# A Fourier filter and a snake MLP on one core: padded alpha rows, more filler matmuls in the head, a denser batch 1, and stores on a third queue

## The chip, the cores and the metric

The kernel runs on 1 core of one Trainium2 chip. The metric is the device time of one execution in microseconds (us), as the median of several runs; lower is better. A core has five engines that run their own instruction streams in order and wait for each other by semaphores: PE (matmuls; its weight loads are shown as PEld), DVE and ACT (element-wise work), POOL (element-wise work, and it issues DMAs) and SP (it only issues DMAs here).

## The reference

`x` holds 8 batches of 3008 rows with 256 channels. The first half filters each channel along the rows in the frequency domain, the second half is an MLP with the snake activation:

```python
X = np.fft.rfft(x, axis=1)
F = (filt_r + 1j * filt_i)[None, :, :]
y = np.fft.irfft(X * F, n=3008, axis=1)
h = y.reshape(24064, 256) @ w_in            # 256 -> 2048
s = np.sin(alpha * h)
g = h + s * s / (alpha + 1e-09)
out = g @ w_out                             # 2048 -> 256
```

Inputs and output are float32.

## The kernel before, in words

**The filter.** The transform of 3008 = 47 x 64 points is done by matmuls in four stages. `first` (L177, tiles `pa`, matmul L180) multiplies by the 47-point table; its result goes through DRAM (`d1`, stored on SP's queue at L185, loaded on POOL's at L192). `forward` (L195, tiles `pb`) multiplies by the 64-point table; ACT copies the result to `xf` (L203). `product` (L210, DVE, L214) and `cross` (L218, DVE, L220 and L221) multiply by the filter; `cross` needs `xs`, the copy of `xf` with its halves swapped, which two DMAs on SP's queue make (L207). `inverse` (L223, tiles `pc`, matmul L231) goes back; its results `g` are stored to `d2` on SP's queue (L238), and `load_t4` (L241, SP's queue, L243) reads them again in another order. `last` (L246, tiles `pd`, matmuls L255 for batch 0 and L258 for the others) ends the transform and leaves `y`, with channels on partitions. There are 12 units `u` of forward, product, cross and inverse, and 16 of `first` and `last`, for each of the 8 batches. `evac` (L156) copies a PSUM tile, on ACT (L159) or DVE (L161): where the caller doesn't say, by turns, two on ACT and one on DVE.

**The MLP.** `hidden` (L498) takes a chunk of up to 512 columns of `y` and one of 16 blocks of 128 hidden channels: two matmuls (L505, tile `ph`, four PSUM buffers), a cosine on ACT (L508), and on DVE `v = cos - 1 - ph` (L509). With `w_in` multiplied by alpha and `w_out` by -1/(2 alpha) beforehand this is the snake. `project` (L513) multiplies `v` by `w_out` (matmuls L521, tile `po`); ACT copies the result to `o` (L527), and `store` (L536) writes rows of `o` to DRAM in two to seven DMAs (L546).

**The order.** There are 48 chunks; batches go in pairs. The main loop (L617) has 8 steps for each chunk and one more chunk's worth at the end: a step issues two `hidden` of chunk k, then whatever of the filter is due, then the `project` units of chunk k-1. What is due is a list `pending` (L552): every piece of the filter is put there with a due time in steps (`put`, L554), sorted, and `slot` (L594) issues what is due, at most one PE piece at a time unless it is a step late. A piece's due time is thus the only thing that says where it lands in each engine's stream.

**The head.** Batch 0's filter is done in a way of its own before the main loop, in an order written by hand (L359 to L490), with the DRAM trips replaced by DVE transposes (`turn`, L381, L383). Three details matter here:

- `spread_alpha` (L293) brings alpha, split by POOL into three bf16 parts (`split_alpha`, L284), to all 128 partitions by matmuls (L298): 12 for each of four tiles, called twice in pairs, as early as L377 and again at L481. `one` and `part` have 16 rows.
- `warm_pe(n)` (L347) issues n matmuls of 128x512 on a tile of zeros (L352). Nothing reads their result.
- The last head pieces are `s0.last(0)`, `(2)`, `(1)`, `(3)`. The first two read `t4_h[0]`, which `turn_back(0)` writes on DVE, the other two `t4_h[1]` from `turn_back(1)`. Eight matmuls make one piece. Chunk 0 needs all four.

```python
    spread_alpha(2)
    spread_alpha(3)
    for step in ([(weights_in, g) for g in range(6)] + [(s1.load_x, 0), (s1.load_x, 1)]):
        step[0](*step[1:])
    warm_pe(2)
    s0.last(0, True)
    s0.last(2, True)
    warm_pe(1)
    s0.last(1, True)
    s0.last(3, False)
```

**The end.** The last chunk has four blocks of 128 columns. Blocks 0 and 1 leave together; blocks 2 and 3 (`final`) are copied and stored alone. SP's queue carries all stores, but for the last two blocks the second piece of a run goes to ACT's queue (L539).

Of the kernel before, what the change touches and what calls it, by code (L numbers as in the profile page):

```python
# [11 lines left out]
BF16 = mybir.dt.bfloat16  # L12
UINT32 = mybir.dt.uint32
AFT = mybir.ActivationFunctionType
ALU = mybir.AluOpType
# [47 lines left out]
def kernel(  # L63
# [10 lines left out]
    nc = tc.nc  # L74
# [17 lines left out]
    def pool(name, bufs, space=None):  # L92
        kw = {} if space is None else {"space": space}
        return ctx.enter_context(tc.tile_pool(name=name, bufs=bufs, **kw))

    cpool = pool("consts", 1)
# [27 lines left out]
    for h in range(2):  # L124
        nc.sync.dma_start(out=x32[:, 4 * C * h:4 * C * h + 4 * C],
                          in_=bass.AP(tensor=x.tensor, offset=x.offset + 4 * h * C, ap=[[32 * C, 96], [1, 4 * C]]))
# [145 lines left out]
    id32 = cpool.tile([16, 16], FP32)  # L272
# [5 lines left out]
    nc.gpsimd.dma_start(out=id16, in_=id16_dram.ap())  # L278
    e1_0 = by_half(t4_h[1])
    rest = cpool.tile([16, 128], FP32)  # L280
    parts = [cpool.tile([16, 128], BF16, name=f"part{i}") for i in range(3)]
    one = cpool.tile([16, 16], BF16)

    def split_alpha():  # L284

        nc.gpsimd.tensor_copy(out=one, in_=id32)
        for i, part in enumerate(parts):
            src = rest if i else al
            nc.gpsimd.tensor_copy(out=part, in_=src)
            if i < 2:  # L290
                nc.gpsimd.tensor_tensor(out=rest, in0=src, in1=part, op=ALU.subtract)

    def spread_alpha(i):  # L293

        ps = hps.tile([128, 4, 128], FP32, name=f"al_bc_{i}", tag="h")
        for a in range(4):
            for k, part in enumerate(parts):
                nc.tensor.matmul(out=ps[:, a, :], lhsT=one[:, 4 * i + a:4 * i + a + 1].to_broadcast([16, 128]),  # L298
                                 rhs=part, start=(k == 0), stop=(k == 2))
        nc.scalar.copy(out=alpha[:, i // 2, 512 * (i % 2):512 * (i % 2) + 512], in_=ps.rearrange("p a b -> p (a b)"))  # L300

    for g in range(2):
        gs = slice(12 * g, 12 * g + 12)
        for k, filt in enumerate((filt_r, filt_i)):
            for q in range(2):
                if (g, k, q) == (0, 1, 1):
                    split_alpha()
                off, step = ((12 * g) * C, C) if q == 0 else ((N1 - 12 * g) * C, -C)
                marks["filt", g, k] = nc.gpsimd.dma_start(
                    out=f_t[k][64 * k + 32 * q:64 * k + 32 * q + 32, gs, :],  # L310
                    in_=bass.AP(tensor=filt.tensor, offset=filt.offset + off,
                                ap=[[N1 * C, 32], [step, 12], [1, C]]))
        nc.gpsimd.dma_start(out=e_t[:, gs, :], in_=e_dram.ap()[:, gs])
# [33 lines left out]
    def warm_pe(n):  # L347

        warmed.append(n)
        ps = hps.tile([128, 512], FP32, name=f"warm_{len(warmed)}", tag="h")  # L350
        for i in range(n):
            nc.tensor.matmul(out=ps, lhsT=idle[:, 0:128], rhs=idle[:, 0:512], start=True, stop=True)  # L352
# [13 lines left out]
    for i in range(16):  # L366
        own, tag = (fps, "f") if i % 3 == 2 else (hps, "h")
        ps = own.tile([128, 512], FP32, name=f"pa_0_{i}", tag=tag)
# [6 lines left out]
        if i < 15 and i % 4 == 3:  # L375
            warm_pe((2, 2, 2, 1)[i // 4])
    spread_alpha(0)  # L377
    spread_alpha(1)
    warm_pe((2, 2, 2, 1)[3])

# [71 lines left out]
    s0 = Spectral(0)  # L452
# [20 lines left out]
    def weights_out(jb, n=4):  # L473
# [3 lines left out]
        else:  # L477
            nc.gpsimd.tensor_tensor(out=w2[:, jb:jb + n, :], in0=w_out32[:, jb:jb + n, :],
                                    in1=rec_t[:, jb:jb + n, None].to_broadcast([128, n, C]), op=ALU.mult)
# [4 lines that stand above are left out]
# [1 line left out]
    warm_pe(2)  # L485
    s0.last(0, True)
    s0.last(2, True)
    warm_pe(1)
    s0.last(1, True)
    s0.last(3, False)  # L490

    chunks = [(pb, c0, 384 if c0 == 2560 else 512) for pb in range(B // 2)
              for c0 in [*range(0, 2561, 512), *range(2944, 2 * S, 512)]]
# [19 lines left out]
    def project(k, u):  # L513

        pb, c0, n = chunks[k]
        t, half = divmod(u, 2)
        final = k == len(chunks) - 1 and t > 1
        if (t % 2 == 0 or final) and half == 0:
            pso[k] = ops.tile([128, 2, C], FP32, name=f"po_{k}_{t}", tag="o")
        for jb in range(8 * half, 8 * half + 8):  # L520
            nc.tensor.matmul(out=pso[k][:, t % 2, :], lhsT=v[k][:, jb, 128 * t:128 * t + 128],  # L521
                             rhs=w2[:, jb, :], start=(jb == 0), stop=(jb == 15))
        last = 128 * (t + 1) == n
        if half == 1 and (t % 2 == 1 or last or final):
            i0 = t % 2 if final else 0
            o = opool.tile([128, 2, C], FP32, name=f"o_{k}_{t}", tag="o")
            nc.scalar.copy(out=o[:, i0:t % 2 + 1, :], in_=pso[k][:, i0:t % 2 + 1, :])  # L527
            for i in range(i0, t % 2 + 1):
                store(o[:, i, :], pb, c0 + 128 * (t - t % 2 + i), final)

    def runs(cnt):

        whole = cnt if max(d for d in range(1, 17) if cnt % d == 0) > 7 else cnt - cnt % 16
        return [(0, whole), (whole, cnt - whole)] if 0 < whole < cnt else [(0, cnt)]

    def store(o_blk, pb, col, final):  # L536

        p = 0
        queues = [nc.sync, nc.scalar] if final else [nc.sync, nc.sync]  # L539
        while p < 128:  # L540
            odd, rest = divmod(col + p, S)
            n2, row = divmod(rest, NR)
            cnt = min(128 - p, NR - row)
            t0 = (2 * pb + odd) * S + 32 * row + n2
            for i, (r0, rows) in enumerate(runs(cnt)):
                queues[i].dma_start(  # L546
                    out=bass.AP(tensor=out.tensor, offset=out.offset + (t0 + 32 * r0) * C,
                                ap=[[32 * C, rows], [1, C]]),
                    in_=o_blk[p + r0:p + r0 + rows, :])
            p += cnt  # L550
# [3 lines left out]
    def put(at, fn, *args, pe=False):  # L554
        pending.append((at, len(pending), pe, fn, args))
# [10 lines left out]
    for i in range(2):  # L566
        put(13 + i, negate, i)
    for u in range(4, 16, 2):
        put((1,2.5,4,6,14,16)[u // 2 - 2], s0.last_two, u, pe=True)
    for b in range(1, B):  # L570
        s = s1 if b == 1 else Spectral(b)
        z = 48 * b
        if b > 1:
            for ch in range(4):
                put((22,27,32,37)[ch] if b == 2 else z - 92 + 7 * ch, s.load_x, ch)
        for i in range(16):
            put(7.5 + 0.3 * i if b == 1 else 36 + 0.66 * i if b == 2 else z - 67 + 0.66 * i, s.first, i, pe=True)
        for g in range(4):
            put(12.5 if b == 1 else max(z - 56, 46.5), s.load_t2, g)
        for u in range(12):  # L580
            inv = 23.5 + 1.3 * u if b == 1 else 59 + 2.1 * u if b == 2 else z - 40.8 + 2.3 * u
            fwd = inv - (6 if b == 1 else 6)
            put(fwd, s.forward, u, pe=True)
            put(fwd + (0.5 if b == 1 else 1.5), s.product, u)
            if s.fused:
                put(fwd + (4 if b == 1 else 4.5), s.cross, u)
            put(inv, s.inverse, u, pe=True)
        for ch in range(4):
            put(z - (9 if b == 1 and ch < 3 else (10.5, 10.5, 10.5, 3)[ch]), s.load_t4, ch)
        for u in range(16):  # L590
            put(z + (u - (4.5 if b == 1 else 6.5) if u < 4 else 2 * u - 9), s.last, u, pe=True)
    pending.sort(key=lambda p: p[:2])

    def slot(at):  # L594
# [22 lines left out]
    for k in range(len(chunks) + 1):  # L617
        for j in range(8):
            if k < len(chunks) and step > 0:
                hidden(k, 2 * j)  # L620
                hidden(k, 2 * j + 1)
            slot(step)
            if k > 0:
                n_half = 2 * (chunks[k - 1][2] // 128)
                for u in range(n_half * j // 8, n_half * (j + 1) // 8):
                    project(k - 1, u)
            slot(step + 0.5)
            step += 1
# [31 lines left out]
```

## Time and profile before

| what | value |
|---|---|
| median of 7 runs | 793.91 us (791.41 to 796.93) |
| the profiled execution | 792.52 us |
| its span, first to last instruction | 790.6 us |
| its mean granted TensorE clock | 0.994 |
| PE busy | 777.6 us |
| DVE busy | 657.8 us |
| ACT busy | 616.8 us |
| POOL busy | 77.8 us |

How to read the views: the page gives busy times by engine, the chain of work that ended last, and groups of instructions by source line. The timeline lists instructions in order of time: start, length, engine, line, operation, `out<-in`, for PE the rows and columns of the array that the weights fill (`16*128`), the partitions x elements that are streamed, a count, and in brackets the idle time of the engine before it and what ended it. Starts are in us from the span's start. The table of windows gives for each stretch the busy time of PE, PEld, DVE, ACT and POOL, then the granted TensorE clock (1.00 is full, 0.50 is half), the busy share of the DMA engines and their GB/s.

### The profile page before, as it was taken

How to read it: one execution, taken by the hardware profiler on the slowest of the kernel's cores; microseconds unless marked ns; L12 is line 12 of the kernel's file. 1: busy time of each engine (PE TensorE's matmuls, PEld its weight loads, DVE VectorE, ACT ScalarE, POOL GpSimd, SP SyncE). 2: the span in 40 equal slices, each digit the busy share in tenths (PEclk: the TensorE clock that was granted, in tenths of full speed). 3: DMA queues.
4: the chain of work that ended last, by engine and by line, in shares of the span. 5: the costliest groups of instructions: out<-in, count | busy, mean ns of one | idle time of the engine just before them, and what ended most of it. 6: DMA issues, size and time to landing. Idle time of an engine off the chain costs nothing.

```text
span 790.6 us, 16719 instructions
## 1 busy us (share of the span) xinstructions
PE 777.6 (98%) x5852; PEld 536.5 (68%) x5852; DVE 657.8 (83%) x1171; ACT 616.8 (78%) x1209; POOL 77.8 (10%) x119
## 2 busy tenths in 40 slices
PE   8999999999999999999999999999999999999997
PEld 4756666676667766776666766777666776766665
DVE  6887997799878997799978998799987999777773
ACT  5787887888878888788787888788887887777663
POOL 5442000200020000200020000200002000000000
PEclk9999999999999999999999999999999999999999
DMA  9955576756573646654475445845556243421111
GB/s 212 259 106 158 113 154 187 189 111 132 139 206 81 125 109 171 170 121 105 112 206 131 101 105 138 221 92 112 129 164 170 61 98 82 116 61 29 41 41 54
DMA packets 87653, 101.01 MB, mean 128 GB/s; under 512 B 14448, under 2 KB 75904, under 8 KB 87568
## 3 DMA queue, kind: packets, MB, share of 16 engines
q1 hardware_dynamic: 78056, 73.75, 34.4%
q0 software_dynamic: 9296, 26.13, 17.3%
q8 instruction: 46, 0.75, 0.4%
q14 instruction: 39, 0.32, 0.1%
q10 hardware_dynamic: 216, 0.05, 0.0%
HBM read 55.72 MB, written 46.66 MB: 129 GB/s over the span
## 4 chain that ended last, share of the span: by engine, by line
PE 88%; DVE 4%; DMA 4%; ACT 2%; issue 1%; SPq 0%; POOL 0%; ACTq 0%; DVEq 0%; POOLq 0%
PE po L521 38%; PE ph L505 38%; PE pa L180 3%; PE pd L258 2%; PE pb L200 2%; PE pc L231 2%; DVE v L509 2%; DMA id<-id 2%; ACT cos_all L508 1%; DMA out_dram<-o 1%; PE pd L255 1%; PE pb L401 1%; DMA d<-g 1%; DVE t_h L383 1%; DMA xs<-xf 0%
## 5 line engine op out<-in xcount | busy, mean ns | idle before, releaser
L509 DVE SCALAR_TENSOR_TENSOR v<-cos_all,ph 128x512 f16<-128x512 f32 (+1 forms) x768 | 483.2, 672 | 109.3 <-ACT cos_all L508 105.5
L508 ACT ACTIVATE cos_all<-ph 128x512 f32<-128x512 f32 (+1 forms) x768 | 411.1, 592 | 100.8 <-PE ph L505 99.6
L505 PE MATMUL ph<-y,w 128*128 128x512 f16 (+1 forms) x1536 | 388.1, 376 | 0.8 <-ACT y L159 0.7
L521 PE MATMUL po<-w,v 128*128 128x256 f16 x3008 | 388.8, 273 | 0.0
L521 PEld LDWEIGHTS <-v 128*128 128x128 f16 x3008 | 289.2, 98 | 78.3 <-issue 1.1
L505 PEld LDWEIGHTS <-w 128*128 128x128 f16 x1536 | 147.6, 98 | 105.5 <-issue 3.8
L527 ACT COPY o<-po 128x512 f32<-128x512 f32 (+1 forms) x97 | 55.6, 573 | 19.6 <-PE po L521 13.4
L203 ACT CAST xf<-pb 128x512 f16<-128x512 f32 x84 | 49.9, 595 | 14.8 <-PE pb L200 12.7
L192 POOL DMA_DIRECT2D t<-d x56 | 36.3, 666 | 208.1 <-DMA out_dram<-o 120.2
L159 ACT CAST t_h<-pa 96x512 f16<-96x512 f32 x76 | 44.5, 586 | 9.5 <-PE pa L180 9.4
L140 POOL DMA_DIRECT2D x<-in_x_dram x32 | 17.1, 537 | 296.7 <-PE pc L231 160.4
L159 ACT CAST y<-pd 128x376 f16<-128x376 f32 x83 | 40.0, 482 | 7.5 <-PE pd L258 5.3
L258 PEld LDWEIGHTS <-t_h 96*128 96x128 f16 x448 | 31.3, 97 | 18.6 <-DMA t_h<-d 0.5
L180 PE MATMUL pa<-x,wf_t 94*96 94x512 f16 x112 | 42.3, 381 | 1.1 <-DVE t_h L161 0.6
L159 ACT CAST g<-pc 128x512 f16<-128x512 f32 x56 | 33.3, 595 | 7.6 <-PE pc L231 7.2
L221 DVE TENSOR_TENSOR p<-p,xs 128x512 f16<-128x512 f16 x84 | 35.7, 425 | 2.9
L258 PE MATMUL pd<-wi_t,t_h 96*128 96x94 f16 x448 | 37.2, 205 | 0.1
L220 DVE TENSOR_TENSOR xs<-xs,filt_t 128x512 f16<-128x512 f16 x84 | 35.1, 418 | 0.7 <-DMA xs<-xf 0.7
L214 DVE TENSOR_TENSOR p<-xf,filt_t 128x512 f16<-128x512 f16 x84 | 35.1, 418 | 0.0
L231 PE MATMUL pc<-p,e_t 128*128 128x256 f16 x168 | 32.1, 273 | 0.4 <-DVE g L161 0.4
L200 PE MATMUL pb<-t,d_t 128*128 128x256 f16 x168 | 32.1, 273 | 0.1
L161 DVE CAST y<-pd 128x376 f16<-128x376 f32 x45 | 24.4, 543 | 0.9 <-PE pd L255 0.9
(63 smaller groups left out, 257.3 us busy)
## 6 DMA issues: line engine op xcount, KB each, us to landing
x<-in_x_dram POOLq DMA_DIRECT2D x30, 376.0 KB, 4.8
d<-t_h SPq DMA_DIRECT2D x28, 384.0 KB
t<-d POOLq DMA_DIRECT2D x56, 192.0 KB, 4.7
xs<-xf SPq DMA_DIRECT2D x168, 64.0 KB
d<-g SPq DMA_DIRECT2D x56, 192.0 KB
t_h<-d SPq DMA_DIRECT2D x28, 384.0 KB
out_dram<-o SPq DMA_DIRECT2D x104, 80.0 KB
w_out<-in_moe_w_out_dram SPq DMA_DIRECT2D x1, 2048.0 KB
```

The source lines that it names most:

```text
L159: marks["act"] = nc.scalar.copy(out=dst, in_=src)
L180: marks["pe"] = nc.tensor.matmul(out=ps[0:NK, :], lhsT=wf_t, rhs=self.x[ch][:, 2 * j:2 * j + 2, :], start=True, stop=True)
L192: nc.gpsimd.dma_start(out=self.t2[g][64 * p:64 * p + 64, :, :], in_=self.d1[a0:a0 + 6, :, :].rearrange("s n c -> n s c"))
L200: nc.tensor.matmul(out=ps[:, i, :], lhsT=d_t[:, s, :], rhs=self.t2[s // 6][:, s % 6, :], start=True, stop=True)
L203: nc.scalar.copy(out=self.xf[u], in_=ps)
L231: nc.tensor.matmul(out=ps[:, i, :], lhsT=e_t[:, 2 * w + i, :], rhs=pt[:, i, :], start=(k == 0), stop=(k == len(pr) - 1))
L258: nc.tensor.matmul(out=psv[:, i, :], rhs=wi_t, start=True, stop=True, lhsT=t4_h[ch // 2][0:NK, n0 % 16 + i, cb * 128:cb * 128 + 128])
L505: nc.tensor.matmul(out=ps[:, 0:n], lhsT=w1[:, cb, jb * 128:jb * 128 + 128], rhs=y_cols[:, cb, c0:c0 + n], start=(cb == 0), stop=(cb == 1))
L508: nc.scalar.activation(out=cs[:, 0:n], in_=ps[:, 0:n], func=AFT.Sin, bias=float(np.pi / 2))
L509: marks["snake"] = nc.vector.scalar_tensor_tensor(out=v[k][:, jb, 0:n], in0=cs[:, 0:n], scalar=-1.0, in1=ps[:, 0:n], op0=ALU.add, op1=ALU. ...
L521: nc.tensor.matmul(out=pso[k][:, t % 2, :], lhsT=v[k][:, jb, 128 * t:128 * t + 128], rhs=w2[:, jb, :], start=(jb == 0), stop=(jb == 15))
L527: nc.scalar.copy(out=o[:, i0:t % 2 + 1, :], in_=pso[k][:, i0:t % 2 + 1, :])
```

## The change

Four edits:

1. `one` and the three `part` tiles get 128 rows instead of 16. POOL sets them to zero first (four new instructions ahead of the filter loads on POOL's queue), and `spread_alpha` multiplies all 128 rows. The added rows are zero.
2. Between the last head pieces `warm_pe(1)` becomes `warm_pe(3)`.
3. Due times in the main loop: for batch 1 the inverse pieces are 1.25 steps apart instead of 1.3 (forward, product and cross go with them), `load_t4` is due half a step earlier, and so are `last` 0 to 3; batch 0's `last` pairs 6 and 8 are due half a step later.
4. `store` takes the second queue as an argument: ACT's for the final blocks as before, POOL's for the last chunk's first two blocks, SP's otherwise.

```diff
-    parts = [cpool.tile([16, 128], BF16, name=f"part{i}") for i in range(3)]
-    one = cpool.tile([16, 16], BF16)
+    parts = [cpool.tile([128, 128], BF16, name=f"part{i}") for i in range(3)]
+    one = cpool.tile([128, 16], BF16)
+    for t in [one] + parts:
+        nc.gpsimd.memset(t, 0.0)
...
-        nc.gpsimd.tensor_copy(out=one, in_=id32)
+        nc.gpsimd.tensor_copy(out=one[0:16], in_=id32)
...
-            nc.gpsimd.tensor_copy(out=part, in_=src)
+            nc.gpsimd.tensor_copy(out=part[0:16], in_=src)
...
-                nc.gpsimd.tensor_tensor(out=rest, in0=src, in1=part, op=ALU.subtract)
+                nc.gpsimd.tensor_tensor(out=rest, in0=src, in1=part[0:16], op=ALU.subtract)
...
-                nc.tensor.matmul(out=ps[:, a, :], lhsT=one[:, 4 * i + a:4 * i + a + 1].to_broadcast([16, 128]),
+                nc.tensor.matmul(out=ps[:, a, :], lhsT=one[:, 4 * i + a:4 * i + a + 1].to_broadcast([128, 128]),
...
     s0.last(2, True)
-    warm_pe(1)
+    warm_pe(3)
     s0.last(1, True)
...
-                store(o[:, i, :], pb, c0 + 128 * (t - t % 2 + i), final)
+                store(o[:, i, :], pb, c0 + 128 * (t - t % 2 + i),
+                      nc.scalar if final else nc.gpsimd if k == len(chunks) - 1 else nc.sync)
...
-    def store(o_blk, pb, col, final):
+    def store(o_blk, pb, col, second):
...
-        queues = [nc.sync, nc.scalar] if final else [nc.sync, nc.sync]
+        queues = [nc.sync, second]
...
-        put((1,2.5,4,6,14,16)[u // 2 - 2], s0.last_two, u, pe=True)
+        put((1,3,4.5,6,14,16)[u // 2 - 2], s0.last_two, u, pe=True)
...
-            inv = 23.5 + 1.3 * u if b == 1 else 59 + 2.1 * u if b == 2 else z - 40.8 + 2.3 * u
+            inv = 23.5 + 1.25 * u if b == 1 else 59 + 2.1 * u if b == 2 else z - 40.8 + 2.3 * u
...
-            put(z - (9 if b == 1 and ch < 3 else (10.5, 10.5, 10.5, 3)[ch]), s.load_t4, ch)
+            put(z - (9.5 if b == 1 and ch < 3 else (10.5, 10.5, 10.5, 3)[ch]), s.load_t4, ch)
...
-            put(z + (u - (4.5 if b == 1 else 6.5) if u < 4 else 2 * u - 9), s.last, u, pe=True)
+            put(z + (u - (5 if b == 1 else 6.5) if u < 4 else 2 * u - 9), s.last, u, pe=True)
```

The order of the changed program differs from the one before in these places only. PE: two more filler matmuls; `hidden` of blocks 6 and 7 of chunk 0 ahead of `last` 6 and 7 of batch 0 instead of behind; and between chunk 2's middle and chunk 6 the batch 1 pieces (and batch 2's `first` around them) up to one piece earlier or later. DVE and ACT follow that, with some `g`, `y` and `t_h` copies changing between the two. POOL: four memsets in the head and two stores at the end. SP: two stores fewer at the end; all else on SP's queue keeps its order.

## The prediction

> **What bounds the kernel.** I read the page first, then the chain of waits, the table of windows for the head, the timelines around PE's gaps, and the end.
>
> ```profile
> PE 777.6 (98%) x5852; PEld 536.5 (68%) x5852; DVE 657.8 (83%) x1171; ACT 616.8 (78%) x1209; POOL 77.8 (10%) x119
> PE 88%; DVE 4%; DMA 4%; ACT 2%; issue 1%; SPq 0%; POOL 0%; ACTq 0%; DVEq 0%; POOLq 0%
> ```
>
> The first line is busy time by engine, the second the chain by engine. PE has 13 us without work, and nothing in the middle can be won but by filling PE's gaps. After 45 us the timeline shows four gaps of over 0.2 us: 0.31 at 52.17, 0.58 at 62.17, 0.41 at 118.94 and 0.66 at 138.97. The rest of the gaps lies in the head and behind PE's end at 785.94. So the change works at three places: head, batch 1, end.
>
> The windows of the head, cut where the granted clock changed:
>
> ```profile
> 13.26:16.67 3.41, 2.88 (x53) 2.26 (x53) 3.08 (x4) 2.13 (x5) 1.39 (x4) 1.00 1.19 209
> 16.67:20.08 3.41, 3.41 (x44) 2.59 (x39) 3.38 (x4) 3.41 (x6) 1.99 (x3) 0.50 1.16 226
> 30.32:33.73 3.41, 3.24 (x50) 2.76 (x49) 2.74 (x2) 2.81 (x6) 2.81 (x2) 1.00 1.05 354
> 33.73:37.15 3.42, 2.89 (x35) 2.19 (x33) 3.10 (x3) 1.78 (x4) 3.42 (x3) 1.00 1.09 349
> 37.15:40.56 3.41, 3.30 (x10) 1.00 (x9) 1.79 (x3) 1.29 (x3) 3.38 (x3) 0.50 0.90 286
> 40.56:43.97 3.41, 3.19 (x30) 2.05 (x29) 2.61 (x7) 2.85 (x6) 1.91 (x3) 1.00 0.26 27
> ```
>
> The third number from the end is the clock. It was half for exactly one window twice, 16.67 to 20.08 and 37.15 to 40.56; all four edges lie on one grid of 3.41 us. PE's busy time doesn't tell why: 2.88 and 2.89 went before a half window, 3.24 and 3.19 did not. What PE did in those windows does:
>
> ```profile
> 32.06 1.51 PE L298 MATMUL al_bc<-part,one 16*128 16x128 bf16 x24
> 33.50 0.61 PE L352 MATMUL warm<-idle 128*128 128x512 f16 x2
> 34.04 1.17 PE L255 MATMUL pd<-wi_t,t_h 128*64 128x94 f16 x16
> 35.14 0.39 PE L352 MATMUL warm<-idle 128*128 128x512 f16 x1
> 36.06 1.17 PE L255 MATMUL pd<-wi_t,t_h 128*64 128x94 f16 x16 [0.53 <-DVE t_h L383]
> 37.16 2.18 PE L505 MATMUL ph<-y,w 128*128 128x512 f16 x4
> 39.49 1.55 PE L505 MATMUL ph<-y,w 128*128 128x512 f16 x4
> ```
>
> A full 128x512 matmul takes 0.216 us in the chain's rows (0.86 for four). I weigh each matmul by columns streamed and by the share of the array its weights fill: `pd` (94 columns, half the array) 0.020 us, `al_bc` (128 columns, 16 of 128 rows) 0.007, a filler 0.216. Then 33.73 to 37.15 holds 32 x 0.020 and one to two fillers, 0.9 to 1.05 us: a share of 0.25 to 0.31. 13.26 to 16.67 comes to about 1.1, 0.33. The weakest windows with no half clock behind them come to 0.49 (30.32) and 0.45 (40.56). Busy time or rows alone don't separate them; this does, with a limit between 0.33 and 0.45. The fillers stream zeros, and the clock was full from 6.43 on after ten of them, so zeros count.
>
> **Edit 1, padding.** An `al_bc` counts 0.054 instead of 0.007, 24 of them 1.14 us more, a third of a window; its time stays (24 in 1.51 us here, and full 128x128 `pc` come every 0.056). The window before 16.67 rises to 0.65, so the first half-clock window should go. That is worth almost nothing: DVE's timeline has no gap of over 0.14 us from 14.38 to 30.83, and its next is
>
> ```profile
> 31.50 4.51 DVE L383 STREAM_TRANSPOSE t_h<-t_h 128x2048 uint32<-128x2048 uint32 x2 [0.67 <-ACT t_h L159]
> ```
>
> so 0 to 0.2, taken as 0. The four memsets stand on POOL before the filter loads. No row has their size; the nearest are POOL's 128x1 memset (0.10) and its 16x128 subtraction (0.42), so 0.4 to 1.7 us, inside the 3.85 us that POOL then waits for a load of x; the loads they delay stand behind 4.8 us of earlier ones. 0.
>
> **Edit 2, fillers.** Two more cost 0.43 in the 0.53 that PE waits for `turn_back(1)`: free, 0.1 to spare. They lift 33.73 to 37.15 to 0.38 to 0.43. The grid's phase belongs to one execution, so I slid a 3.41 window over the rows: before, every start from 31.1 to 34.9 is below 0.38, so any phase meets it; after, with the padding, the lowest is 0.41 to 0.43 for starts from 33.6 to 34.8 (a third of the phases), 0.45 or more elsewhere. I take the half window as gone. Its price stands in the chain: from the end of DVE's `y` copy at 37.83, three `ph` took 1.46 instead of 0.65, a transpose 0.22 (0.12 at full clock), four `ph` 1.48 instead of 0.86: **1.5 us**. Behind it, PE's next steps wait for ACT's `y` copies (0.56 at 44.31); moving pairs 6 and 8 frees that wait, since `pd` 7 then takes a buffer that DVE emptied, and puts one of the same kind in front of `pd` 9: 0, with 0 to 0.5 of the 1.5 lost again for the range. POOL's weights are done by 40.53 (31 to 40.5, six of them), blocks 14 and 15 are multiplied at 50: not late. The loads of x for batch 1 start at 42.05 and land 4.8 us later; `pa` would need them at 50.6 instead of 52.17: not late.
>
> The Trainium skill, "TensorE: Matmul & The Clock Gate", Part 1, speaks against both edits: it says that the clock falls back only after an idle window of about 3.4 us. PE never idled that long here, so by the page the edits bring 0 and the sum below would be 0.9, 791.6 us. The windows above decide against it: the clock fell to 0.50 after 2.89 us of busy PE.
>
> **Edit 3, batch 1.** The two gaps:
>
> ```profile
> 117.41 0.42 DVE L220 TENSOR_TENSOR xs<-xs,filt_t 128x512 f16<-128x512 f16 x1 [0.72 <-DMA xs<-xf]
> 118.94 0.38 PE L231 MATMUL pc<-p,e_t 128*128 128x256 f16 x2 [0.41 <-DVE g L161]
> 138.97 0.81 PE L505 MATMUL ph<-y,w 128*128 128x512 f16 x3 [0.66 <-ACT y L159]
> ```
>
> At 138.97 chunk 6 waits for the `y` copy of `last` 3, which ACT does behind the copy of `o`. Half a step earlier, `last` 3 stands in front of eight `po` (0.87) and the copy in front of `o`: -0.66. Its data comes earlier too, since `inverse` 11 now leaves by ACT and not behind DVE's queue (121.20). At 118 it gets worse. DVE runs without a gap from 84.77 to 116.68, and a `ph` starts 0.05 us after the `v` that frees its buffer at 114.94. The denser order puts `cross` 11 in front of two pairs' worth of `v`, so DVE comes to it at 115.4; its `xs` landed at 117.31, and SP's queue, in unchanged order and without a pause from 100.42, can't bring that forward by more than 0.6. Inverse 11 then waits from 117.3 to 118.25 if nothing lands earlier, to 117.65 if 0.6 earlier: 0.35 to 0.95, and 0.2 to 0.3 for the `ph` behind, against 0.46 now: 0.1 to 0.8 lost, taken as 0.4. Edit 3: **-0.25**, from -0.6 to +0.5.
>
> **Edit 4, stores.** The end:
>
> ```profile
> 785.98 0.37 ACT L527 COPY o<-po 128x256 f32<-128x256 f32 x1 [1.38 <-DMA out_dram<-o]
> 787.07 0.80 SPq L546 DMA_DIRECT2D out_dram<-o  x2
> ```
>
> The last copy is done at 786.35, but SP issues its stores at 787.07, being late with 17 stores from 779.97 on, 0.46 each. Two fewer give 0.9; the copy allows 0.68: **-0.68**. POOL's two issue from 783.1; its issues take 0.67 at most and land 4.8 us later at worst, 789.2, before SP's last now (789.25). So 0 to -0.68.
>
> **Sum.** 0 - 1.5 - 0.25 - 0.68 = -2.4: 790.1 us against the profiled execution's 792.52 (span 790.6). That one is 1.4 below the median, 793.91. If the scatter (791.41 to 796.93) comes mostly from where the half windows fall, which in other phases can follow each other, the change takes that away too, and the median is 790.1; if not, 791.5. I take the middle, **790.8**.
>
> **Rivals.**
> - *The gate stays*: padded zero rows don't count, or 0.41 is too little. For it: 0.38 to 0.43 lies inside the unknown stretch. Against: zero fillers count. 793.91 - 0.25 - 0.68 = 793.0. Chance 0.17.
> - *`xs` is late*: at 118 PE waits the full 0.95 + 0.3 and ACT, which now meets `xf` 11 before two cosines, waits for its buffer too (1.4 us were waited for that once, at 103.85). +1.3 on the forecast: 792.1. Chance 0.13.
> - *The head's 1.5 us is swallowed*: ACT and DVE each have some 11.7 us of work in the 15 us from 38 on, and the waits for `y` grow. 1.1 lost: 791.9. Chance 0.10.
> - *Slower than before*: the gate closes on the window before 36 and stays closed for three, since a half-clock window can't count over 0.5 and 37.15 to 40.56 had only 0.44. Three times 1.53, and three fillers at half clock take 1.29 in the 0.92 from 35.14 to 36.06, 0.37 late: 5.0 on 791.5, 796.5. It needs a share under 0.33 there. Chance 0.05.
>
> The forecast keeps 0.55. About 0.3%, 2.4 us, is what a measurement of this kernel can tell from no change: faster is under 791.5, slower over 796.3. Forecast: faster; first three rivals: same (0.40); the last: slower. 8 in 10: from 789.4 (0.7 gained at 118 as well, scatter gone) to 793.4 (the gate stays).
>
> **What would show it.** The clock at 1.00 in every window from 6.43 to PE's end; the first `ph` after `y` 0.216 apart; PE done with `pd` 4 some 1.5 us earlier; no gap before chunk 6's first `ph`; a gap of 0.3 to 1.0 before inverse 11; SP's last two stores right behind the last copy. A clock of 0.50 near 37, or a gap over 1.5 us near 118, would make it wrong.

## The result and the profile after

| | before | after |
|---|---|---|
| median | 793.14 us (49 runs) | 790.6 us (788.54 to 792.83, 19 runs) |
| ratio, 95% interval | | 0.9961 (0.9951 to 0.9971): -3.1 us (-3.9 to -2.3) |
| the profiled execution | 792.52 us | 789.73 us |
| its span, mean clock | 790.64 us, 0.994 | 787.94 us, 0.999 |

Predicted were 790.8 us and, for the pair of profiled executions, -2.4; measured were 790.6 us and, for the pair, -2.79. The two medians differ by 2.5 us, inside the interval of the ratio. The page of the changed kernel, PE's line and the chain by engine:

```profile
PE 775.4 (98%) x5854; PEld 535.9 (68%) x5854; DVE 657.9 (83%) x1171; ACT 616.6 (78%) x1209; POOL 79.6 (10%) x125
PE 90%; DMA 3%; DVE 3%; ACT 1%; SPq 1%; issue 1%; POOL 0%; ACTq 0%; DVEq 0%; POOLq 0%
```

PE does two more matmuls in 2.2 us less: it no longer runs at half clock. The windows at the places that were shown of before (third number from the end: the clock):

```profile
13.26:16.67 3.41, 2.64 (x58) 2.31 (x56) 3.21 (x4) 2.22 (x4) 1.29 (x3) 1.00 1.20 196
16.67:20.08 3.41, 3.26 (x36) 2.23 (x36) 3.31 (x4) 3.41 (x6) 1.56 (x3) 1.00 1.13 210
33.73:37.15 3.42, 3.13 (x36) 2.32 (x36) 2.95 (x3) 1.55 (x4) 3.42 (x3) 1.00 1.09 349
37.15:40.56 3.41, 3.09 (x25) 1.65 (x24) 2.30 (x5) 2.41 (x5) 3.41 (x3) 1.00 1.06 333
```

The timeline of PE there. All 24 `al_bc` fill 128 rows, three fillers stand in the gap, and the four `ph` from 38.59 on take 1.04 us, where the four from 39.49 on took 1.55 before:

```profile
31.74 1.50 PE L300 MATMUL al_bc<-part,one 128*128 128x128 bf16 x24
...
34.73 0.82 PE L354 MATMUL warm<-idle 128*128 128x512 f16 x3
35.83 1.20 PE L255 MATMUL pd<-wi_t,t_h 128*64 128x94 f16 x16 [0.29 <-DVE t_h L385]
36.97 0.39 PE L507 MATMUL ph<-y,w 128*128 128x512 f16 x1
37.68 0.82 PE L507 MATMUL ph<-y,w 128*128 128x512 f16 x3 [0.32 <-DVE y L161]
...
38.59 1.04 PE L507 MATMUL ph<-y,w 128*128 128x512 f16 x4
```

In batch 1 the 0.66 before chunk 6 is gone. Before inverse 11 PE waited 0.41; now it comes at 116.60 and waits 0.12, under the 0.2 from which waits are counted here, though DVE still waits 0.32 for `xs` 11. Two waits of PE are new: 0.21 before inverse 10, and 0.38 at 103.81:

```profile
113.04 0.39 PE L231 MATMUL pc<-p,e_t 128*128 128x256 f16 x2 [0.21 <-DVE p L221]
...
114.50 0.42 DVE L220 TENSOR_TENSOR xs<-xs,filt_t 128x512 f16<-128x512 f16 x1 [0.32 <-DMA xs<-xf]
...
116.60 0.38 PE L231 MATMUL pc<-p,e_t 128*128 128x256 f16 x2
```

The end. The last copy is done at 784.08; SP still issues until 785.47, and its last two issues begin 0.59 us behind the copy (0.72 before):

```profile
777.34 8.13 SPq L549 DMA_DIRECT2D out_dram<-o  x16
...
781.09 1.04 POOL L549 DMA_DIRECT2D out_dram<-o  x2 [182.00 <-ACT o L529]
...
783.71 0.37 ACT L529 COPY o<-po 128x256 f32<-128x256 f32 x1 [1.37 <-DMA out_dram<-o]
```

16 issues took 8.13 us, almost as long as 18 before (8.26): one of them, at 780.09, took 1.29 instead of 0.36.

### The profile page after: what moved, and what is told of

Read it like the earlier page. It is cut to its first block, busy times and chain, and to the rows that moved or that the text cites. A ratio compares the mean times of both kernels' runs of the same rounds, so it can differ in the third digit from the quotient of the medians.

```text
span 787.9 us, 16730 instructions
## 1 busy us (share of the span) xinstructions
PE 775.4 (98%) x5854; PEld 535.9 (68%) x5854; DVE 657.9 (83%) x1171; ACT 616.6 (78%) x1209; POOL 79.6 (10%) x125
## 4 chain that ended last, share of the span: by engine, by line
PE 90%; DMA 3%; DVE 3%; ACT 1%; SPq 1%; issue 1%; POOL 0%; ACTq 0%; DVEq 0%; POOLq 0%
PE po L523 40%; PE ph L507 39%; PE pa L180 3%; PE pd L258 2%; PE pb L200 2%; PE pc L231 2%; DMA d_t<-d_tbl 2%; DMA filt_t<-in_filt_i_dram 1%; DVE v L511 1%; SPq L549 1%; PE pd L255 1%; ACT cos_all L510 1%; DVE t_h L385 1%; DMA xs<-xf 0%; DVE t_h L161 0%
## 5 line engine op out<-in xcount | busy, mean ns | idle before, releaser
L200 PE MATMUL pb<-t,d_t 128*128 128x256 f16 x168 | 32.1, 273 | 0.5 <-DVE g L161 0.4
L231 PE MATMUL pc<-p,e_t 128*128 128x256 f16 x168 | 32.1, 273 | 0.3 <-DVE p L221 0.2
L161 DVE CAST t_h<-pa 96x512 f16<-96x512 f32 x38 | 25.8, 680 | 0.7 <-PE pa L180 0.5
```

The costliest lines, as they stand in the source:

```text
L200: nc.tensor.matmul(out=ps[:, i, :], lhsT=d_t[:, s, :], rhs=self.t2[s // 6][:, s % 6, :], start=True, stop=True)
L231: nc.tensor.matmul(out=ps[:, i, :], lhsT=e_t[:, 2 * w + i, :], rhs=pt[:, i, :], start=(k == 0), stop=(k == len(pr) - 1))
```

## The experiments

**How they were read.** A single part of the change is worth about what an interval of a comparison is wide. So besides the times I divided each profiled execution into three stretches: from the first `al_bc` of the head's end (near 31) to batch 1's first `pa`, from there to PE's end, and from PE's end to the end of the span. The first holds edits 1 and 2, the second edit 3, the third edit 4.

| profile of | half windows near 37 | `al_bc` to `pa` | `pa` to PE's end | PE's end to span's end | runs against before, us |
|---|---|---|---|---|---|
| before | 1 | 20.11 | 733.78 | 4.69 | |
| only_pad | 0 | 19.19 | 734.40 | 5.42 | -1.0 (-2.1 to +0.1) |
| only_fill | 0 | 18.91 | 734.69 | 4.96 | -0.8 (-1.7 to +0.1) |
| only_head | 0 | 18.99 | 734.22 | 4.68 | -0.8 (-1.7 to +0.1) |
| only_stores | 2 | 20.50 | 734.32 | 3.71 | -1.0 (-1.7 to -0.2) |
| no_batch1 | 0 | 19.15 | 734.02 | 4.02 | -2.5 (-3.6 to -1.3) |
| only_batch1 | 3 | 22.25 | 732.96 | 5.90 | +0.5 (-0.2 to +1.3) |
| only_rest | 2 | 20.51 | 734.83 | 4.93 | +0.5 (-0.6 to +1.6) |
| after | 0 | 19.07 | 732.86 | 4.27 | -3.1 (-3.9 to -2.3) |
| after_again | 0 | 19.10 | 732.92 | 3.97 | -3.1 (-4.1 to -2.0) |
| x_early | 0 | 19.08 | 736.08 | 4.72 | -1.3 (-2.0 to -0.6) |
| next_try | 0 | 19.07 | 732.83 | 3.84 | -5.1 (-6.5 to -3.6) |

The last column is ratio minus one, with its interval, times the median of before in the same comparison. The first `al_bc` itself starts anywhere from 30.1 to 32.1.

**only_pad**, edit 1 alone (`one` and `part` with 128 rows).

```diff
-    parts = [cpool.tile([16, 128], BF16, name=f"part{i}") for i in range(3)]
+    parts = [cpool.tile([128, 128], BF16, name=f"part{i}") for i in range(3)]
```

> The kernel before with the padding alone. Theory (the clock is granted by the share of the array that a 3.41-us window fills, zeros included): the window before 16.67 rises from 0.33 to about 0.65, so the half-clock window at 16.67 goes and the one at 37 stays; as DVE is never late there, the time stays: 0 to -0.2 us, with a mean clock of about 0.996 against 0.994. Rival 1 (padded zero rows do not count, or the clock falls only after an idle window): both half-clock windows stay, 0 us. Rival 2 (the four memsets hold up loads in the head): +0.4 to +1.7 us.

Measured 0.9987 (0.9974 to 1.0001). The window near 16 is gone, as the theory had it. One profile would not show that, since it is also missing in two of the five profiles without padding (only_stores and only_rest), but it is missing in all seven with padding. In this execution the window near 37 is gone too: the 24 padded `al_bc` stand right before it, and with this phase (31.39 to 34.80, 34.80 to 38.21) no window is weak enough. Its runs have mean clocks from 0.994 to 1.0, so it does not go in all of them. The padded rows count, then, and here the stretch to `pa` is 0.9 us shorter; that edit 1 alone is worth more than 0 in the times stays open, as the interval reaches +0.1.

**only_fill**, edit 2 alone.

```diff
-    warm_pe(1)
+    warm_pe(3)
```

> The kernel before with three fillers instead of one, without padding. Theory: 33.7 to 37.1 rises from 0.25 to 0.31 to 0.38 to 0.43, inside the unknown stretch of 0.33 to 0.45, so the half-clock window at 37 goes in some executions or in all: -0.5 to -1.5 us; the one at 16.67 stays. Rival 1 (the page's idle rule): 0 us, both windows stay. Rival 2 (the gain is swallowed by ACT's copies of y): the window goes, and yet 0 to -0.4 us.

Measured 0.999 (0.9978 to 1.0001): the middle is of the theory's size, the interval reaches 0. Half clock from 15.92 to 19.34, none near 37. The stretch to `pa` is 18.91, the shortest of all: ACT's copies of `y` swallow nothing here.

**only_head**, edits 1 and 2.

```diff
+    parts = [cpool.tile([128, 128], BF16, name=f"part{i}") for i in range(3)]
+    warm_pe(3)
```

> The kernel before with padding and three fillers, without the new due times and stores. Theory: no half-clock window, mean clock 0.999 or 1.0, pd 4 starts about 1.4 us earlier, and the time is 1.5 us shorter (1.3 to 1.9). Rival (most of the 3.1 us that the whole change gives comes from batch 1 and the stores, since these two alone show 0.66 + 0.41 + 0.43 of vanished idle time): -1.0 us or less here, and -1.5 to -2 with those two alone.

Measured 0.999 (0.9978 to 1.0001), in the middle about half of what was expected, though the clock is full; the interval, -1.7 to +0.1, holds the expected -1.5. The profile has a wait, the first of these two, that before's profile does not have:

```profile
128.32 0.34 PE L258 MATMUL pd<-wi_t,t_h 96*128 96x94 f16 x4 [0.77 <-DMA t_h<-d]
...
136.53 0.81 PE L507 MATMUL ph<-y,w 128*128 128x512 f16 x3 [0.66 <-ACT y L159]
```

Five of the six profiles with the old due times (all but before's) have this wait for `t_h`, 0.60 to 1.08 us; none of the six with the new ones has it. The wait thus goes with the old due times and not with the head: only_stores has it with the old head. That it took part of the gain here is not shown, as most executions of the kernel before may have it too. Counted from the first `pc` of batch 1, SP starts the last stores of `d` 33.8 us later here and the reads of `t_h` 39.1; in the changed kernel 31.1 and 34.8.

**only_rest**, edits 3 and 4.

```diff
+            inv = 23.5 + 1.25 * u if b == 1 else 59 + 2.1 * u if b == 2 else z - 40.8 + 2.3 * u
+        queues = [nc.sync, second]
```

> The kernel before with the new due times and the stores on three queues, without padding and fillers. By the prediction -0.25 - 0.68 = -0.9 us; from the rows of the changed kernel (gaps of 0.66 at 138.97 and 0.41 at 118.94 gone, 0.2 and 0.4 new ones, 0.43 at the end) -0.9 to -1.3. Mean clock 0.994 as before, both half-clock windows there. Rival (the earlier head is what let batch 1's xs land in time): the gap before inverse 11 grows to 0.4 to 0.95 us here and the sum is -0.5 to +0.1.

Measured 1.0006 (0.9992 to 1.002): not the theory; the rival's -0.5 to +0.1 lies in the interval. The profile shows the rival's late `xs`, with 1.35 us before inverse 11:

```profile
117.16 0.43 DVE L220 TENSOR_TENSOR xs<-xs,filt_t 128x512 f16<-128x512 f16 x1 [2.71 <-DMA xs<-xf]
...
118.10 0.39 PE L231 MATMUL pc<-p,e_t 128*128 128x256 f16 x2 [1.35 <-DVE p L221]
```

The later head explains little of it: SP issued `xs` 11 at 110.83 here and at 110.23 in the changed kernel, and it landed 2.7 us later. The load of x that POOL issued at 108.87 took 7.33 us (4.78 there). With it, half clock lasted two windows, 33.97 to 40.79.

**after_again**, the changed kernel once more, unedited, beside its parts.

> The changed kernel once more, beside runs of its parts on one chip. The parts measured so far do not add up (head alone -0.6, due times and stores alone +1.0 beside medians of before), against -3.1 for the whole. Theory 1 (the parts help each other: with the head alone batch 1's first last pieces wait 0.77 to 1.08 us for t_h near 128, which earlier load_t4 removes): again -2.5 to -3.5 us. Theory 2 (the parts add, and the first comparison was a lucky draw from a scatter of 4 us): -0.5 to -1.8 us.

Measured 0.9961 (0.9948 to 0.9975): the first comparison was no lucky draw. DVE waits 0.83 for `xs` 11 here, of which 0.12 reach PE at inverse 11; PE waits 0.78 at 101.95 for ACT's `xf`.

**only_batch1**, edit 3 alone.

```diff
+            inv = 23.5 + 1.25 * u if b == 1 else 59 + 2.1 * u if b == 2 else z - 40.8 + 2.3 * u
+            put(z + (u - (5 if b == 1 else 6.5) if u < 4 else 2 * u - 9), s.last, u, pe=True)
```

> The kernel before with the new due times alone. Theory: at 118 PE waits for inverse 11 as long as its xs is late, 0 to 1.4 us by the load of x that is under way then (it took 4.8 us in the changed kernel, 7.3 us where PE waited 1.35), and the 0.66 before chunk 6 is gone: -0.6 to +0.7 us. By the prediction -0.25. Rival (denser is simply better): -1.0 us or more.

Measured 1.0006 (0.9997 to 1.0016), within the theory's range; its own stretch is short (732.96). This profile has what the prediction priced as the slower rival, in a kernel with one filler: half clock for three windows in a row, and 22.25 us to `pa` instead of 19.1:

```profile
31.95:35.36 3.41, 3.06 (x39) 2.18 (x36) 3.41 (x2) 2.41 (x5) 3.41 (x3) 1.00 1.06 361
35.36:38.78 3.42, 3.14 (x20) 1.44 (x21) 1.60 (x4) 1.07 (x2) 3.42 (x3) 0.50 1.10 349
38.78:42.19 3.41, 3.41 (x23) 1.84 (x23) 2.67 (x6) 2.27 (x4) 1.48 (x2) 0.50 0.44 141
42.19:45.60 3.41, 3.41 (x10) 0.97 (x8) 2.07 (x5) 1.79 (x3) 3.11 (x4) 0.50 0.51 67
45.60:49.02 3.42, 2.85 (x34) 2.12 (x33) 2.75 (x5) 2.60 (x5) 3.41 (x3) 1.00 0.99 176
```

**only_stores**, edit 4 alone.

```diff
-        queues = [nc.sync, nc.scalar] if final else [nc.sync, nc.sync]
+        queues = [nc.sync, second]
```

> The kernel before with the last chunk's stores on three queues alone. By the prediction -0.68 us; by the changed kernel's profile -0.43, since SP's issue at 780.09 took 1.29 us there and SP was again late; -0.68 if that issue is short here. From PE's end to the end of the span: 4.0 to 4.25 us instead of 4.69. Rival (POOL's landings or its wait at the end hold the end): 0 or a loss.

Measured 0.9988 (0.9978 to 0.9997), -1.0 us in the middle; from PE's end to the span's end it takes 3.71, less than the expected 4.0 to 4.25. No issue is long here, and SP's last two begin 0.02 us behind the last copy (785.88):

```profile
779.14 7.59 SPq L547 DMA_DIRECT2D out_dram<-o  x16
...
785.51 0.37 ACT L527 COPY o<-po 128x256 f32<-128x256 f32 x1 [1.37 <-DMA out_dram<-o]
```

From the last copy's end to the span's end, without a long issue: 4.27 to 4.55 before the edit (three profiles), 3.30 to 3.60 with it (three): -0.9. With a long issue of 1.3 to 1.7 us: 5.01 and 5.49 before it, 3.86, 4.30 and 4.52 with it.

**gate_probe**, behind the changed kernel 14 stages of matmuls that nothing reads.

```diff
+    for stage in STAGES:
+        for i in range(40):
+            probe(128, 128)
+        for i in range(stage[0]):
+            for args in stage[1:]:
+                probe(*args)
```

> The changed kernel, and behind its last project 14 stages of matmuls that nothing reads, each behind 40 full 128x512 matmuls; its time is longer by these. Stages of 12 us at full clock. Theory (array share, limit between 0.33 and 0.45): full clock for 64 rows x 128 columns (0.50), 128 x 64 (0.50), zeros in the full array (1.0) and 128x64-element full matmuls; half clock after one window for 40 rows (0.31), 32 rows (0.25), 128 x 32 (0.25), 64 x 64 (0.25) and one full with four of 16 rows (0.30); 56 rows (0.44), 48 rows and 128 x 48 (0.375), and mixes of 0.42 and 0.34 narrow the limit. Rival 1 (rows count, columns do not): all stages of 128 rows at full clock, 64 x 64 too. Rival 2 (busy time or the page's idle rule): every stage at full clock. Rival 3 (zeros do not count): half clock in the stage of zeros.

Windows inside the stages of 64, 56 and 48 rows (its first window, then the rest), 128x64, 128x32, 64x64, one full with two of 16 rows (its last window at full clock, then the rest), and zeros, in this order:

```profile
793.00:805.00 12.00, 12.00 (x56) 5.08 (x55) 0.00 (x0) 0.00 (x0) 0.00 (x0) 1.00 0.00 1
814.00:825.90 11.90, 11.90 (x56) 5.05 (x54) 0.00 (x0) 0.00 (x0) 0.00 (x0) 1.00 0.00 0
837.10:840.40 3.30, 3.30 (x17) 1.46 (x16) 0.00 (x0) 0.00 (x0) 0.00 (x0) 1.00 0.00 0
840.50:853.00 12.50, 12.50 (x30) 4.14 (x28) 0.00 (x0) 0.00 (x0) 0.00 (x0) 0.50 0.00 0
...
926.00:938.20 12.20, 12.20 (x58) 6.07 (x57) 0.00 (x0) 0.00 (x0) 0.00 (x0) 1.00 0.00 0
...
968.00:980.00 12.00, 12.00 (x56) 5.24 (x54) 0.00 (x0) 0.00 (x0) 0.00 (x0) 1.00 0.01 1
988.90:1001.00 12.10, 12.10 (x56) 5.81 (x57) 0.00 (x0) 0.00 (x0) 0.00 (x0) 1.00 0.00 1
1010.82:1014.23 3.41, 3.41 (x13) 0.81 (x12) 0.00 (x0) 0.00 (x0) 0.00 (x0) 1.00 0.00 0
1014.60:1032.90 18.30, 18.30 (x38) 2.73 (x36) 0.00 (x0) 0.00 (x0) 0.00 (x0) 0.50 0.00 0
1113.00:1124.60 11.60, 11.60 (x55) 5.29 (x54) 0.00 (x0) 0.00 (x0) 0.00 (x0) 1.00 0.01 1
```

PE is shown busy without a pause in every stage. With 48, 40 and 32 rows the clock fell after one whole window of the grid; with 56 and more it stayed. Columns do not count: 128x32 and even 64x64, both a quarter of the array, keep the full clock. My measure by array share is wrong; rival 1, rows, is right, and busy time is out. Zeros count. The mixed stage needs care: its matmuls do not follow each other every 0.216 us. In the trace a group of three starts every 0.855 us, not every 0.65, and 13 matmuls lie in its window from 1010.82, where 17 of 48 rows do in 837.10 to 840.40. So its share is (0.216 + 2 x 0.027) / 0.855 = 0.32 and not 0.417, and that it fell fits the streams: 40 rows, 0.31, fell too.

**gate_probe2**, eleven further stages, among them two column halves in turn.

```diff
+        [(28, (128, 64), (128, 64, 512, 64, 1))],
+        [(40, (32, 128)), (40, (96, 128))], [(40, (32, 128)), (40, (112, 128))], [(40, (32, 128)), (40, (104, 128))]]
```

> The changed kernel and 11 stages behind it, as in the first probe, which showed that columns do not count in a stream of one column half, and a limit between 0.417 and 0.4375 for rows times time. 52 rows (0.41): half clock; 54 rows (0.42): near the limit. Theory (two matmuls in the two column halves run side by side and count once): 128x64 alternating halves with 512 elements takes about 0.11 us each and stays at full clock; as pd does it (94 elements, alternating halves) the count is rows times the time of a pair, and the clock falls where 0.039 us per pair is under 0.42 of the time that a pair takes. Rival (array share after all, or a count that columns enter in some other way): the alternating 512 stage takes 0.216 each and keeps the full clock, and pd's stage keeps it as well. Last three stages, 32 rows and then 96, 112 and 104 rows without a full stage between: if the limit is the same absolute count at half clock, 96 rows (0.375 at half clock) stay at half clock, 112 (0.4375) come back to full, 104 (0.41) stay; if the limit goes with the clock, all three come back.

52 and 54 rows kept the full clock. For 52 the expectation was wrong: its limit of 0.417 came from the mixed stage, taken as if its matmuls came every 0.216 us. A stream's limit lies between 48 and 52 rows of 128 (0.375 and 0.41). Two 64-column halves in turn: 57 matmuls in 6.1 us, 0.11 each instead of 0.22. They run side by side:

```profile
792.10:804.20 12.10, 12.10 (x56) 5.11 (x56) 0.00 (x0) 0.00 (x0) 0.00 (x0) 1.00 0.01 1
...
833.90:840.00 6.10, 6.10 (x57) 3.08 (x56) 0.00 (x0) 0.00 (x0) 0.00 (x0) 1.00 0.00 0
...
939.80:943.10 3.30, 3.30 (x9) 1.21 (x8) 0.00 (x0) 0.00 (x0) 0.00 (x0) 0.50 0.00 0
943.20:949.50 6.30, 6.30 (x30) 2.84 (x29) 0.00 (x0) 0.00 (x0) 0.00 (x0) 1.00 0.00 0
```

The last two lines: at half clock, one window of 96 rows (0.375 of what full clock could do) brought the full clock back; 104 and 112 rows did so too. The expectation had put down all three coming back to a limit that goes with the clock, half of 0.41. But in only_batch1 the window at half clock from 35.36 on (x20: 16 `pd` and four `ph`) comes to 16 x 0.020 + 4 x 0.216 = 1.18 us of 3.41, an estimate of 0.35, and half clock stayed. So the limit at half clock lies near 0.35 to 0.375, about the same absolute amount of work, as the slower rival reckoned. The stage shaped like `pd` kept its clock, but its pairs came every 0.042 us and those of `pd` come every 0.12, so it says nothing on the limit for `pd`.

**no_batch1**, the changed kernel with the old due times.

```diff
-            inv = 23.5 + 1.25 * u if b == 1 else 59 + 2.1 * u if b == 2 else z - 40.8 + 2.3 * u
+            inv = 23.5 + 1.3 * u if b == 1 else 59 + 2.1 * u if b == 2 else z - 40.8 + 2.3 * u
```

> The changed kernel with the old due times: padding, fillers and stores only. Stretches read from the profiles so far: from the first al_bc of the head's end to batch 1's first pa 18.9 to 19.2 us, from there to PE's end 734.2 to 734.7 (the five profiles with old due times show 733.8 to 734.7, those with new ones 732.9 three times and 734.8 once), from PE's end to the span's end 3.7 to 4.3; gaps of about 0.8 before pd near 127 and 0.66 before chunk 6. Theory (the new due times are worth about -1.3 us beside the shorter head): -1.3 to -2.2 us against the kernel before, where the whole change gave -3.1. Rival (the new due times are worth nothing, as they were alone, +0.5): -2.5 us or more here.

Measured 0.9968 (0.9954 to 0.9983): the middle, -2.5 us, is the rival's number, and the interval, -3.6 to -1.3, holds the theory's as well; the times do not settle it. The stretch is 734.02, with 0.60 waited for `t_h` at 128 and 0.66 before chunk 6: the theory's profile. One profile does not decide it.

**x_early**, batch 2's loads of x ahead of batch 1's traffic.

```diff
-                put((22,27,32,37)[ch] if b == 2 else z - 92 + 7 * ch, s.load_x, ch)
+                put((14,16,18,20)[ch] if b == 2 else z - 92 + 7 * ch, s.load_x, ch)
```

> The changed kernel with batch 2's four loads of x due at steps 14, 16, 18 and 20 instead of 22, 27, 32 and 37, so that none is under way when xs 11 and the reads of t_h are. Theory (xs 11 and t_h come late where a load of x shares the DMA engines: its 1.35 us at 116.8 came with a load that took 7.3 us): DVE's wait for xs 11 (0.32 and 0.83 in the two profiles of the changed kernel) goes under 0.2, and the time is 0.2 to 0.8 us below the changed kernel's, so -3.3 to -3.9 against the kernel before. Rival 1 (SP's own queue of stores holds them): the wait stays and the time too, -3.1. Rival 2 (the loads now collide with the first xs and t2 of batch 1): a new gap between 85 and 100, +0.5 us or more.

Measured 0.9984 (0.9975 to 0.9993), 1.8 us worse than the changed kernel: rival 2. The loads took 7.3 to 9.4 us each; `xs` 11 no longer waits, but earlier ones do:

```profile
83.72 0.42 DVE L220 TENSOR_TENSOR xs<-xs,filt_t 128x512 f16<-128x512 f16 x1 [1.91 <-DMA xs<-xf]
...
87.26 0.38 PE L200 MATMUL pb<-t,d_t 128*128 128x256 f16 x2 [0.51 <-ACT xf L203]
```

The `xs` that waits at 83.72 was issued by 75.59 and landed 8.1 us later, with four loads of x under way. So loads of x under way delay `xs`; where to put them was guessed wrongly.

**next_try**, those loads behind `xs` 11, and POOL as second queue for one chunk more.

```diff
-                      nc.scalar if final else nc.gpsimd if k == len(chunks) - 1 else nc.sync)
+                      nc.scalar if final else nc.gpsimd if k >= len(chunks) - 2 else nc.sync)
-                put((22,27,32,37)[ch] if b == 2 else z - 92 + 7 * ch, s.load_x, ch)
+                put((22,30,35.5,39)[ch] if b == 2 else z - 92 + 7 * ch, s.load_x, ch)
```

> The changed kernel with two further edits, read apart by stretches: batch 2's second, third and fourth load of x due at steps 30, 35.5 and 39 instead of 27, 32 and 37 (behind xs 11 and behind the first reads of t_h), and POOL as second queue for the last two chunks' stores instead of the last one's. Theory for the loads (a load of x under way delays xs 11 and t_h): no wait of DVE for xs 11 over 0.2 us near 114, and from batch 1's first pa to PE's end 732.9 us or a little less (732.9, 732.9, 733.0 and 734.8 with the new due times so far; 736.1 where the loads came earlier). Rival: the loads now meet batch 2's first pa or the stores of d, with a new gap of 0.5 us or more behind 115. Theory for the stores (SP comes late to the last chunk because single issues of 1.3 to 1.7 us push it back, which happened in 6 of 11 profiles): from the end of the last copy to the end of the span 3.3 to 3.6 us in any case, instead of 3.3 to 3.6 or 3.9 to 4.5. Rival: POOL's stores land late and hold the end, 4 us or more. Whole: 0.2 to 0.8 us below the changed kernel, -3.3 to -3.9 against the kernel before.

Measured 788.45 us, 0.9936 (0.9918 to 0.9955): -5.1 us, faster than both kernels. (Long issues of SP were in 5 of the 11 profiles, not 6.) Its six runs lie between 788.28 and 788.74, where the changed kernel's 25 spread from 788.3 to 792.8. The profiled stretches are those of the changed kernel's good case, 732.83 and 3.84; DVE comes to `xs` 11 without a wait:

```profile
113.26 0.42 DVE L220 TENSOR_TENSOR xs<-xs,filt_t 128x512 f16<-128x512 f16 x1
```

All ten profiles with the third load of x in its old place, the kernel before included, have a wait of DVE for `xs` 11, 0.30 to 2.71 us; the two with it moved, x_early and this, have none. By its six runs the two edits make the best case the usual one rather than a better one. How much each does was not tried.

## Why the prediction was right, and where it was not

The mechanisms came out in the main; the hit to 0.2 us is partly luck, since a step too large, one too small and a middle chosen without a measurement made it up. The profiled pair, by stretches: -0.32 before the first `al_bc`, -1.04 to `pa`, -0.92 to PE's end, -0.42 behind it, together the span's -2.70.

- **Edit 1, 0.** The half window near 16 went, as said; but the padding also props up the window before 37, where it meets it (only_pad). In the times edits 1 and 2 cannot be told apart; each alone removes half or more of the half windows. By mean clocks (one half window is 3.41 x 0.5 / 790 = 0.0022), an execution has 2.6 of them before, 1.0 with the padding alone, 1.3 with the fillers alone, 0.6 with both in only_head, and 0.4 after. These counts take in half clock behind PE's end, which costs nothing: in before's profile the clock is half from 788.08 on, which counts as 0.75 of a window, and in only_head's 0.62 and the changed kernel's 0.23 are all there is.
- **Edit 2, -1.5.** Mechanism right, size too large for this pair: -1.04. The `ph` that wait for `y` come 5.94 us behind the first `al_bc` instead of 5.82, and from them to `pa` 1.16 is gained, 0.34 less than the three rows said. For the median it is too small, since of the four profiles with this part of the head unchanged three have two or three half windows in a row there: 20.5 and 22.3 us to `pa`. All eight with padding or fillers have none.
- **The measure.** Array share gave the right windows for a partly wrong reason. What counts is rows times streaming time, not columns. That `pd` had to be weighed by half fits with its two column halves running side by side: in before's trace the matmuls of `pd` start in pairs, at most 8 ns apart, a pair every 0.12 us. On the rule of the Trainium skill, "TensorE: Matmul & The Clock Gate", Part 1: the clock fell in a stream of 48 rows in which PE never idled, so the measurement decides against an idle window as the only cause.
- **Edit 3, -0.25.** The 0.66 went. At 118 the loss of 0.4 did not come: the gap of 0.3 to 1.0 before inverse 11 that the prediction gave as a sign is 0.12, where 0.41 was. SP issued `xs` 11 2.2 us earlier than before, 0.8 more than the head's gain, where I allowed 0.6. What the step did not see is the wait for `t_h` near 128: before's profile is the one old-order execution without it, and load_t4 was costed only by what it moves. The middle stretch is 732.8 to 733.0 in four profiles with the new due times and 734.8 in one (x_early apart), against 733.8 to 734.7 (mean 734.2) in six with the old ones. So about -1.4 where `xs` 11 is at most 0.83 late for DVE, and +0.6 where it is 2.71 late. The times do not show that gain: only_batch1 and only_rest both measured +0.5. By their mean clocks they have 3.2 and 2.7 half windows against 2.7 and 2.3 for the kernel before beside them, which by the fit below is 0.3 to 0.4 us of it; whether edit 3 causes them is open. Of this pair's -0.92, PE's gaps over 0.2 us give -0.48 (-0.66 - 0.41 + 0.38 + 0.21); where the rest lies was not traced.
- **Edit 4, -0.68.** -0.9 by the profiles without a long issue, -1.0 (-1.7 to -0.2) by the times alone. So -0.68 was somewhat small. The -0.42 of this pair goes with one long issue of SP, and the last two stores, which should have stood right behind the last copy, begin 0.59 behind it.
- **The median.** The prediction took half of the scatter for half windows. In a fit over all timed executions, in which each kernel has a mean of its own in each comparison, one half window goes with 0.8 us (plus or minus 0.2), so 2.6 less 0.4 of them are worth 1.8 us, an estimate, as part of that difference lies behind PE's end. But executions of the changed kernel at clocks of 0.999 and 1.0 still spread from 788.3 to 792.2. The rest may be `xs` and `t_h` landing late and SP's long issues; next_try, which keeps both from mattering, has a narrow spread in its six runs. The middle was a choice, and the sum around it came out: -3.1 is about -1.8 from the clock, -0.9 from the end, and what is left for batch 1 is -0.4; the times alone do not measure that last part.
- **Rivals.** The clock stayed full; that copies of `y` swallowed part of the head's gain no profile shows. The late `xs` is real and came in only_rest. The three closed windows came in only_batch1: that mechanism is real, it cost 3.2 us there (22.25 against 19.07) instead of 5.0, and it belongs to the head before the change.

## What to carry to other kernels

A granted clock of one half can follow a window in which the engine was busy throughout: look at how many rows the matmuls fill and how closely they follow each other, and pad thin ones with zero rows or put full fillers into waits. When a part alone gives nothing and the whole gives something, first compare the difference with the intervals, then divide the executions into stretches and look for a wait that only some of them have. And one profile shows one draw of the DMA traffic: a wait that it lacks may be there in most executions.

## What the runs showed of the hardware that was not expected

- The clock's count ignores columns: 64x64 kept full clock, 48x128 lost it after one window of 3.41 us.
- Matmuls into the two column halves, in turn, took 0.11 us each instead of 0.22.
- SP's DMA issues take 0.3 to 0.6 us each, but 31 of 889 before and 38 of 887 after took 0.9 to 1.8, and one over 1.2 falls among the last 18 in five of twelve profiles. What makes them long was not tried.
- One full matmul in turn with two of 16 rows took 0.855 us a group instead of 0.65, three times 0.216.
- A load of x (376 KB) in the main loop took 4.4 to 9.4 us from issue to landing; the longest, 7.3 to 9.4, include the four that x_early issued within 7 us.
